# Feed-forward: late w_out tiles split one at a time, the first late piece a unit earlier, and the order of the slots' last copies

## The chip, the cores and the metric

One core of one Trainium2 chip runs the whole program; the other cores are idle. The metric is the device time of one execution in microseconds (us). The kernel before was timed three times: 435.57, 437.71 and 440.0 us, median 437.71 us.

## The reference, cut to what matters

Three layers follow one another. Sizes: batch 4, 8 heads, 768 steps, head width 48, so 3072 tokens of width 384; 32 slots (8 experts of 4), expert width 1024; network width 2048. All data are float32, and `w_in`, `w_out` of the last layer arrive as 64-bit floats.

```python
# 1 linear attention with decay, per batch and head
y[t] = r[t] @ (state + (u*k[t]) v[t]^T);  state = w * state + k[t] v[t]^T
# 2 soft mixture of experts on the tokens x (3072 x 384)
logits = x @ phi
d = softmax of logits over tokens (with + 1e-09 in the sum);  slot_input = d.T @ x
slot_out = relu(slot_input[e] @ w1[e]) @ w2[e]               # 4 slots per expert
x = (softmax of logits over slots) @ slot_out
# 3 feed-forward network with ELU
h = x @ w_in                                                 # 3072 x 2048
g = where(h > 0, h, exp(min(h, 0)) - 1)
out = g @ w_out                                              # 3072 x 384
```

## The kernel before, in words

Each engine has a queue of instructions that it works off in order. The kernel sets that order itself: the program text is the order, and semaphores are put in wherever one engine needs another's result. TensorE (PE) multiplies, VectorE (DVE) and ScalarE (ACT) do the elementwise work, GpSimd (POOL) a part of it, SyncE (SP) issues nearly all transfers.

**Attention and slots.** Tokens go by in 24 chunks of 128. Four chunks make a group, and for each of six groups `slots_a` to `slots_f` work up the logits `lg` (32 slots by 4 chunks, as 128 partitions by 128 columns): a running maximum `nmx`, the exponential `el`, its transposition back to tokens (`slots_c`, `slots_d`, giving `et`), the product with the tokens (`slots_e`, `ps_s`), and the rescaled sum `pall` (`slots_f`). The last group has its own order, `last_part` (L773). After its exponentials, `combine_a` (L792) copies the four chunk rows' running minima of `nmx` side by side (`m3`), reduces them (`mm`), copies the result back to four groups of partitions (`nm`, four copies) and lets ScalarE take `sc = exp(-nmx + nm)`. Then come the transposition `slots_c`, VectorE's copy `et`, ScalarE's copy `el` of the logits (`slots_g`), VectorE's `rb = sc * i3` (`combine_c`), the product `ps_s`, the sums `pl`, the second transposition and the combination `pi` (`combine_b`). A few filler products (`warm`) stand between them on TensorE. The experts' two products and the split of the first 10 of 16 row tiles of w_out follow.

**The network.** The slot outputs are first multiplied by w_in, so that a hidden tile is one product of the transposed slot weights `cT` with `mst` (`hid`, L1261). Work goes in 48 units. A unit is one block of 512 tokens (6 blocks) and two hidden tiles of 128: first, for all blocks, the tiles 0 to 9 (units 0 to 29), then, for all blocks, 10 to 15 (units 30 to 47). In the loop's pass n the engines get work of neighbouring units:

- TensorE: two hidden products of unit n (`hid`), the second half of the output products of unit n - 3, the first half of those of unit n - 2 (`outp`).
- ScalarE: `tanh` and `expo` of unit n, `upper` of unit n - 1, which rounds the ELU's result to `gh`.
- VectorE: `neg` of unit n, `lower` of unit n - 1 (`gl` = result less `gh`), `elu` of unit n.

The output product has three terms, `gh` by `wh`, `gh` by `wl` and `gl` by `wh` (L1306, L1307, L1309), where `wh` is a rounded tile of w_out and `wl` what rounding took away. A unit has 24 such products of 384 columns. Four PSUM tiles `fo` collect a block's rows; `leave` (L1237) takes them away when a block's last unit is done: ScalarE copies the first pass to `acc`, and in the second pass ScalarE copies to `os` and GpSimd adds, or, for the last four row tiles, VectorE adds and SP stores.

**Late pieces.** The rest of w_in and w_out is loaded and narrowed from 64 to 32 bits during the network, in 12 pieces of 384 columns, the first six of w_in, the last six w_out's tiles 10 to 15 (into `wo2`). A piece takes two units, listed in `steps` (L1359): in its first, two copies on ScalarE (`wide_a`, L314, L315) and two steps on VectorE (`wide_b1`, `wide_b2`, L318, L323); in its second, two steps on VectorE (`wide_b3`, `wide_c`, L329, L334) and two on GpSimd (`wide_d`, L337, L338), and then the load of the piece after the next. `steps` runs from unit 6, without the units in `PAUSE` (12 and 22). In unit 22 the late columns of w_in are multiplied by the slot outputs (`columns`). `SPLIT` (26, 30, 33) names the units in which two late w_out tiles are split at once (`late_split`, L1328): ScalarE's rounding `wh` (L1331) behind `upper` and the piece's copies, VectorE's subtraction `wl` (L1332) ahead of `neg`.

Of the kernel before, what the change touches and what calls it, by code (L numbers as in the profile page):

```python
# [8 lines left out]
F32 = mybir.dt.float32  # L9
# [4 lines left out]
ALU = mybir.AluOpType  # L14
# [222 lines left out]
def kernel(  # L237
# [14 lines left out]
    nc = tc.nc  # L252
    B, H, S, D = r.shape
    E, DM, FE = w1.shape
    NT = B * S
# [12 lines left out]
    FA = 10  # L268
# [28 lines left out]
    for a in range(2):  # L297
# [5 lines left out]
        out=mask, in_=mask, compare_op=ALU.is_gt, fill=0.0, base=0, pattern=[[1, 128]], channel_multiplier=-1  # L303
# [78 lines left out]
    GS = NCH // G  # L382
    nmx = const.tile([GP, GS], F32, name="nmx")
# [14 lines left out]
    with ExitStack() as actx:  # L398
# [22 lines left out]
        def warm(n):  # L421
            ps = pt_p.tile([128, 4, 128], F32, tag="pt", name="warm")
            for i in range(n):
                nc.tensor.matmul(out=ps[:, i % 4, :], lhsT=ident, rhs=ident, start=True, stop=True)
# [269 lines left out]
        def slots_a(j, copy=True):  # L694
            ps = lg[j]
            el = at3.tile([GP, 2, 128], F32, tag="el", name="el", bufs=1)
            al = at3.tile([GP, 1], F32, tag="al", name="al", bufs=2)
            lg[j], wt[j], wt[j, 1] = el, al, el[:, 1, :]
            nj = nmx[:, j:j + 1]
            if j:  # L700
                nc.vector.tensor_reduce(out=al, in_=ps[:GP], axis=AX.X, op=ALU.max)
                nc.vector.tensor_scalar(
                    out=nj, in0=al, scalar1=-1.0, scalar2=nmx[:, j - 1:j], op0=ALU.mult, op1=ALU.min
                )
            else:
                nc.vector.tensor_reduce(out=nj, in_=ps[:GP], axis=AX.X, op=ALU.max, negate=True)
            lg[j, 0] = ps
            if copy:
                slots_g(j)

        def slots_g(j):
            nc.scalar.copy(out=wt[j, 1], in_=lg[j, 0][:GP])

        def slots_b(j):
            el, ps, nj = lg[j], lg[j, 0], nmx[:, j:j + 1]
            nc.scalar.activation(out=el[:, 0, :], in_=ps[:GP], func=ACTF.Exp, bias=nj, accum_out=zz[:, j:j + 1])
            if j:
                nc.scalar.activation(out=wt[j], in_=nmx[:, j - 1:j], func=ACTF.Exp, scale=-1.0, bias=nj)

        def slots_c(j, parts=(0, 1)):  # L720
            ps = pm_p.tile([128, 2, G, NS], F32, tag="pm", name="ps_e")
            for s in parts:
                nc.tensor.transpose(
                    out=ps[:, s].rearrange("p g c -> p (g c)"), in_=lg[j][:, s, :], identity=ident[:GP, :GP]
                )
            lg[j, 2] = ps

        def slots_d(j, parts=(0, 1)):
            ps = lg.pop((j, 2))
            if 0 in parts:  # L730
                wt[j, 0] = at3.tile([128, G, NS], F32, tag="et", name="et", bufs=1)
                nc.vector.tensor_copy(out=wt[j, 0], in_=ps[:, 0])
            if 1 in parts:
                nc.scalar.copy(out=c_sb[:, G * j:G * j + G, :], in_=ps[:, 1])

        def slots_e(j):
            sp = pm_p.tile([128, DM], F32, tag="pm", name="ps_s")
            for g in range(G):
                nc.tensor.matmul(
                    out=sp[32 * g:32 * g + 32, :], lhsT=wt[j, 0][:, g, :], rhs=xs.pop(G * j + g), start=True, stop=True  # L740
                )
            lg[j, 1] = sp
# [30 lines left out]
        def last_part(j):  # L773
            slots_a(j, False)
            slots_b(j)
            combine_a()
            warm(4)
            extra()
            slots_c(j, (0,))
            warm(2)  # L780
            slots_d(j, (0,))
            slots_g(j)
            combine_c()
            slots_e(j)
            slots_f(j)
            slots_c(j, (1,))
            warm(2)
            combine_b()
            slots_d(j, (1,))


        def combine_a():  # L792
            nl = nmx[:, GS - 1:GS]
            for g in range(G):
                nc.vector.tensor_copy(out=m3[:, g:g + 1], in_=nl[32 * g:32 * g + 32, :])
            nc.vector.tensor_reduce(out=mm, in_=m3, axis=AX.X, op=ALU.min)
            for g in range(G):
                nc.vector.tensor_copy(out=nm[32 * g:32 * g + 32, :], in_=mm)
            nc.scalar.activation(out=sc, in_=nl, func=ACTF.Exp, scale=-1.0, bias=nm)

        def combine_c():
            nc.vector.tensor_scalar(out=rb, in0=i3[:GP], scalar1=sc, scalar2=None, op0=ALU.mult)

        def combine_b():
            pi = pt_p.tile([128, KD, 32], F32, tag="pt", name="pi")
            for kk in range(KD):
                nc.tensor.matmul(out=pi[:, kk, :], lhsT=pl[kk], rhs=rb, start=True, stop=True)
            nc.vector.tensor_copy(out=si, in_=pi)
            nc.vector.tensor_tensor(out=zt, in0=sc, in1=zr, op=ALU.mult)
# [74 lines left out]
        def extra():  # L884
            if extras:
                extras.pop(0)()
# [92 lines left out]
    whl = {}  # L979
# [47 lines left out]
    for a in range(2):  # L1027
        for q in range(4):
# [3 lines left out]
                out=s3, in_=s3, compare_op=ALU.is_ge, fill=0.0, base=-spe * e, pattern=[[1, NS]],  # L1032
# [3 lines left out]
                out=s3, in_=s3, compare_op=ALU.is_ge, fill=0.0, base=spe * e + spe - 1, pattern=[[-1, NS]],  # L1036
# [91 lines left out]
    whl = [[we_p.tile([128, 8, DM], F32R, tag="we", name=f"w{x}{g}") for x in "hl"] for g in range(2)]  # L1128
# [32 lines left out]
    wo2 = we_p.tile([128, FB, DM], F32, tag="we", name="wo2")  # L1161
# [28 lines left out]
    def columns(c, n):  # L1190
        return through(c, n, fo_p.tile([128, 512], F32, tag="fo", name="phm"))
# [11 lines left out]
    NPB = NPI + FB  # L1203
# [30 lines left out]
    N, NA = len(units), NB * FA // 2  # L1234
    gh, gl, po, done = {}, {}, {}, []

    def leave(n=1):  # L1237
        for _ in range(n):
            if done:
                o, r, second = done.pop(0)  # L1240
                a = acc[r // 8][:, r % 8, :]
                if not second:
                    nc.scalar.copy(out=a, in_=o)  # L1243
                    continue
                if r < NT // 128 - 4:
                    os_ = f2.tile([128, DM], F32, tag="os", name="os", bufs=4)
                    nc.scalar.copy(out=os_, in_=o)  # L1247
                    nc.gpsimd.tensor_tensor(out=a, in0=os_, in1=a, op=ALU.add)  # L1248
                else:
                    nc.vector.tensor_tensor(out=a, in0=o, in1=a, op=ALU.add)  # L1250
                nc.sync.dma_start(out=out[128 * r:128 * r + 128, :], in_=a)


# [71 lines left out]
                        term(n, i, t, (x,))  # L1325
        gh.pop(n), gl.pop(n)

    def late_split(f):  # L1328
        a, b = (t[:, f % 8:f % 8 + 2, :] for t in whl[f // 8])
        w = wo2[:, f - FA:f - FA + 2, :]  # L1330
        nc.scalar.copy(out=a, in_=w)  # L1331
        nc.vector.tensor_tensor(out=b, in0=w, in1=a.bitcast(F32), op=ALU.subtract)  # L1332

    def both(f, n, s=slice(0, 2)):
        if 0 <= n < N:
            f(n, s)
# [17 lines left out]
        upper(u, tb)  # L1354
        expo(n, tb)

    PAUSE = (12, 22)
    SPLIT = (26, 30, 33)
    steps = [n for n in range(6, N) if n not in PAUSE][:2 * NPB]  # L1359

    hid(0)
    m3, m2 = columns(1024, 128), columns(512, 256)
# [30 lines left out]
    for n in range(2, N + 3):  # L1393
        if n < N:
            hid(n)
        if n <= NARROW:
            narrow(n)
        else:
            if n == NARROW + 1:
                neg(n - 1, slice(0, 2))  # L1400
                lower(n - 2, tb)
                elu(n - 1, slice(0, 2))
            leave(1 if done and done[0][1] % 4 == 0 else 2)
            both(tanh, n)
            leave()
            both(expo, n)
            both(upper, n - 1)
            j, h = divmod(steps.index(n), 2) if n in steps else (-1, 0)
            if h == 0:
                late_wide(j, wide_a)  # L1410
            if n in SPLIT:
                late_split(FA + 2 * SPLIT.index(n))
            both(neg, n)
            both(lower, n - 1)
            both(elu, n)
            for f in (wide_b3, wide_c, wide_d) if h else (wide_b1, wide_b2):
                late_wide(j, f)
        if n < HALF:
            outp_first(n - 2, early if n == 2 else ())
        else:  # L1420
            if n > HALF:
                outp(n - 3, (2, 3))
            if n == PAUSE[1]:
                leave(2)
                m = columns(CA, CB // 2)
                for f in (high, low):
                    for i in range(2):
                        f(*m, i)
            if n - 2 < N:
                outp(n - 2, (0, 1))  # L1430
# [37 lines left out]
```

## Time and profile before

| What | Value |
|---|---|
| median of three runs | 437.71 us |
| the profiled execution's own time | 437.46 us |
| its span, first to last instruction | 435.3 us |
| mean granted clock of TensorE, share of full speed | 0.992 |
| busy TensorE, products / weight loads | 405.7 / 355.9 us |
| busy VectorE / ScalarE / GpSimd | 357.8 / 269.7 / 159.9 us |

All rows below are of this one execution, and times in them are microseconds from the start of the span. Busy time is the sum over an engine's instructions; an instruction's duration can overlap the next one's on the same engine by a little. A wait in brackets is idle time of the engine just before the row's first instruction, with the engine, tile and line that ended it.

### The profile page before, as it was taken

To read this page: it belongs to the slowest core of one execution; us is meant where nothing else is said; L and a number is where in the kernel's file an instruction comes from. 1 tells how busy PE (TensorE), PEld (TensorE's weight loads), DVE (VectorE), ACT (ScalarE), POOL (GpSimd) and SP (SyncE) were. 2 spreads that over 40 slices of the span, in tenths; PEclk is the share of its full clock that TensorE was granted. 3 is DMA by queue.
4 is the path that set the end of the run, shared out by engine and by line. 5 is a ranking of instruction groups with operands and counts; after the bars stand their busy time and mean duration, and the time that the engine had idled before them with its cause. 6 is when DMAs were issued, how large, how long until landed. Compare 5 with 4: busy or idle time off the path is not lost.

```text
span 435.3 us, 10332 instructions
## 1 busy us (share of the span) xinstructions
PE 405.7 (93%) x4177; PEld 355.9 (82%) x4177; DVE 357.8 (82%) x573; ACT 269.7 (62%) x496; POOL 159.9 (37%) x170
## 2 busy tenths in 40 slices
PE   6998989999999979988999999999999899999994
PEld 5777777787777853457989999998989889999994
DVE  5998987999899645669889999997988988777762
ACT  3654654566464411657696878776778767767750
POOL 2365655565656207200004513530314124433340
PEclk9999989999999999999999999999999999999998
DMA  8989999999998886900001111110111002111122
GB/s 155 232 267 274 250 264 259 253 285 270 289 283 252 268 273 220 356 5 0 2 0 38 36 38 36 38 44 30 38 36 38 0 2 72 56 55 48 63 75 80
DMA packets 85097, 57.44 MB, mean 132 GB/s; under 512 B 65328, under 2 KB 76848, under 8 KB 85040
## 3 DMA queue, kind: packets, MB, share of 16 engines
q1 hardware_dynamic: 84224, 56.64, 45.2%
q8 instruction: 35, 0.57, 0.6%
q14 instruction: 22, 0.18, 0.1%
q10 hardware_dynamic: 816, 0.05, 0.1%
HBM read 51.96 MB, written 4.72 MB: 130 GB/s over the span
## 4 chain that ended last, share of the span: by engine, by line
PE 65%; DVE 17%; DMA 6%; ACT 5%; issue 5%; SPq 1%; POOL 1%; DVEq 0%; ACTq 0%; POOLq 0%
PE fo L1306 12%; PE fo L1309 12%; PE fo L1307 12%; PE fh L1261 4%; PE ps_a L582 4%; DMA vd<-in_v_dram 4%; PE py L657 3%; DVE ex L1275 3%; DVE ex L1280 2%; PE pd L1070 2%; PE ph L1048 2%; DVE rT L547 2%; PE py L643 2%; PE ps_k L533 2%; PE ps_r L533 2%
## 5 line engine op out<-in xcount | busy, mean ns | idle before, releaser
L1306 PE MATMUL fo<-wh,gh 128*128 128x384 f32 x384 | 130.3, 339 | 1.5 <-ACT gh L1288 1.0
L1307 PE MATMUL fo<-wl,gh 128*128 128x384 f32 x384 | 129.8, 338 | 0.0
L1309 PE MATMUL fo<-wh,gl 128*128 128x384 f32 x384 | 125.5, 339 | 3.3 <-DVE gl L1291 3.3
L1275 DVE SCALAR_TENSOR_TENSOR ex<-ex,th 128x1024 f32<-128x1024 f32 (+1 forms) x52 | 61.1, 1174 | 20.5 <-ACT ex L1272 20.3
L1306 PEld LDWEIGHTS fo<-wh,gh 128*128 128x128 f32 x384 | 72.2, 188 | 6.0 <-ACT acc L1243 2.4
L1309 PEld LDWEIGHTS fo<-wh,gl 128*128 128x128 f32 x384 | 71.8, 188 | 4.2 <-DVE gl L1291 4.2
L1269 ACT ACTIVATE th<-fh 128x1024 f32<-128x1024 f32 (+1 forms) x53 | 50.3, 950 | 38.3 <-PE fh L1261 38.3
L1307 PEld LDWEIGHTS fo<-wl,gh 128*128 128x128 f32 x384 | 72.2, 188 | 1.8
L1291 DVE TENSOR_TENSOR gl<-ex,gh 128x1024 fp32r<-128x1024 f32 (+1 forms) x52 | 68.4, 1315 | 1.7 <-ACT gh L1288 1.3
L337 POOL TENSOR_TENSOR cv<-raw,cv 128x384 f32<-128x384 f32 x12 | 19.4, 1617 | 132.3 <-ACT gh L1288 51.2
L1280 DVE SCALAR_TENSOR_TENSOR ex<-ex,fh 128x1024 f32<-128x1024 f32 (+1 forms) x52 | 58.8, 1132 | 0.5 <-ACT ex L1272 0.4
L1272 ACT ACTIVATE ex<-fh 128x1024 f32<-128x1024 f32 (+1 forms) x53 | 50.3, 949 | 9.6 <-DVE gl L1291 9.2
L1288 ACT CAST gh<-ex 128x1024 fp32r<-128x1024 f32 (+1 forms) x52 | 51.4, 988 | 6.3 <-DVE ex L1280 4.9
L1248 POOL TENSOR_TENSOR acc<-os,acc 128x384 f32<-128x384 f32 x20 | 26.9, 1359 | 43.8 <-ACT os L1247 43.8
L631 POOL TENSOR_TENSOR bv<-vd,bs 128x384 f32<-128x384 f32 x24 | 24.3, 1011 | 39.9 <-ACT bs L626 39.9
L586 DVE TENSOR_TENSOR am<-ps_a,mask 128x512 f32<-128x512 f32 x48 | 32.5, 681 | 2.4 <-PE ps_a L582 2.1
L1261 PE MATMUL fh<-cT,mst 128*128 128x512 f32 x96 | 30.6, 400 | 1.8 <-DVE mst L1188 1.1
L582 PE MATMUL ps_a<-rT,kT 64*128 64x128 f32 x384 | 28.3, 288 | 0.3 <-ACT kT L556 0.3
L657 PE MATMUL py<-vd,am 128*64 128x48 f32 x768 | 27.8, 226 | 0.4 <-DVE am L586 0.4
L657 PEld LDWEIGHTS py<-vd,am 128*64 128x64 f32 x768 | 25.4, 142 | 0.9 <-DVE am L586 0.7
L556 ACT COPY kT<-ps_k 128x512 f32<-128x512 f32 x24 | 14.1, 586 | 18.1 <-PE ps_k L533 18.1
L582 PEld LDWEIGHTS ps_a<-rT,kT 64*128 64x128 f32 x384 | 23.7, 191 | 1.7 <-ACT kT L556 0.4
(172 smaller groups left out, 650.2 us busy)
## 6 DMA issues: line engine op xcount, KB each, us to landing
we<-in_moe_w_dram SPq DMA_DIRECT2D x14, 768.0 KB, 7.7
we<-in_moe_w_dram SPq DMA_DIRECT2D x16, 512.0 KB, 6.5
rw<-in_r_dram SPq DMA_DIRECT2D x12, 384.0 KB, 5.0
rk<-in_k_dram SPq DMA_DIRECT2D x24, 192.0 KB, 4.7
vd<-in_v_dram SPq DMA_DIRECT2D x24, 192.0 KB, 5.3
out_dram<-acc SPq DMA_DIRECT2D x24, 192.0 KB, 1.9
we<-in_moe_w_dram SPq DMA_DIRECT2D x16, 256.0 KB, 6.0
scr<-in_moe_w_out_dram SPq DMA_DIRECT2D x10, 384.0 KB, 6.1
```

What stands on the lines that cost most here:

```text
L582: nc.tensor.matmul(out=aps[a][:, p, :], lhsT=kT[q, p, :], rhs=rT[n][q, p, :], start=True, stop=True)
L657: nc.tensor.matmul(out=py[q:q + 64, h, :], lhsT=am[n, a][:, p, q:q + 64], rhs=vd[n][:, h, :], start=(c == 0), stop=(c == 0 or h == H - 1),)
L1261: nc.tensor.matmul(out=ph[n][:, i, :], lhsT=mst[(f + i) // 8][:, 128 * ((f + i) % 8):128 * ((f + i) % 8) + 128], rhs=cT[:, TB * blk:TB * b ...
L1269: nc.scalar.activation(out=th[n][:, s], in_=ph[n][:, s], func=ACTF.Tanh, scale=0.5)
L1272: nc.scalar.activation(out=ex[n][:, s], in_=ph[n][:, s], func=ACTF.Exp)
L1275: nc.vector.scalar_tensor_tensor(out=ex[n][:, s], in0=ex[n][:, s], scalar=1.0, in1=th[n][:, s], op0=ALU.add, op1=ALU.mult)
L1280: nc.vector.scalar_tensor_tensor(out=ex[n][:, s], in0=ex[n][:, s], scalar=0.0, in1=ph[n][:, s], op0=ALU.min, op1=ALU.max)
L1288: nc.scalar.copy(out=gh[n][:, s], in_=ex[n][:, s])
L1291: nc.vector.tensor_tensor(out=gl[n][:, s], in0=ex[n][:, s], in1=gh[n][:, s].bitcast(F32), op=ALU.subtract)
L1306: nc.tensor.matmul(out=o, lhsT=gh[n][:, i, s], rhs=wh, start=(f == first), stop=False)
L1307: nc.tensor.matmul(out=o, lhsT=gh[n][:, i, s], rhs=wl, start=False, stop=False)
L1309: nc.tensor.matmul(out=o, lhsT=gl[n][:, i, s], rhs=wh, start=False, stop=(f == final))
```

## The change

It has four parts. `late_split` becomes `late_high` and `late_low`, one tile each: the rounding of tiles 10 to 15 on ScalarE in units 23, 25, 27, 29, 31 and 33, the subtraction on VectorE in units 24, 26, 28, 30, 32 and 33, now behind `elu` instead of ahead of `neg`. `steps` begins at unit 5, and 7 joins the pauses, so that the first piece is worked on in units 5 and 6 instead of 6 and 7; all others stay. In `last_part` the four copies `nm` and the exponential `sc` become `combine_d`, behind the copy `et`; `slots_e` is written ahead of `combine_c`, which are on different engines. The last row tile of the output is added and stored in two halves of 192 columns, the first on SP's queue, the second on ScalarE's.

```diff
--- before.py
+++ after.py
@@ -779,9 +779,10 @@
             slots_c(j, (0,))
             warm(2)
             slots_d(j, (0,))
+            combine_d()
             slots_g(j)
+            slots_e(j)
             combine_c()
-            slots_e(j)
             slots_f(j)
             slots_c(j, (1,))
             warm(2)
@@ -794,6 +795,9 @@
             for g in range(G):
                 nc.vector.tensor_copy(out=m3[:, g:g + 1], in_=nl[32 * g:32 * g + 32, :])
             nc.vector.tensor_reduce(out=mm, in_=m3, axis=AX.X, op=ALU.min)
+
+        def combine_d():
+            nl = nmx[:, GS - 1:GS]
             for g in range(G):
                 nc.vector.tensor_copy(out=nm[32 * g:32 * g + 32, :], in_=mm)
             nc.scalar.activation(out=sc, in_=nl, func=ACTF.Exp, scale=-1.0, bias=nm)
@@ -1246,8 +1250,14 @@
                     os_ = f2.tile([128, DM], F32, tag="os", name="os", bufs=4)
                     nc.scalar.copy(out=os_, in_=o)
                     nc.gpsimd.tensor_tensor(out=a, in0=os_, in1=a, op=ALU.add)
+                elif r < NT // 128 - 1:
+                    nc.vector.tensor_tensor(out=a, in0=o, in1=a, op=ALU.add)
                 else:
-                    nc.vector.tensor_tensor(out=a, in0=o, in1=a, op=ALU.add)
+                    for i, q in enumerate((nc.sync, nc.scalar)):
+                        c = slice(DM // 2 * i, DM // 2 * i + DM // 2)
+                        nc.vector.tensor_tensor(out=a[:, c], in0=o[:, c], in1=a[:, c], op=ALU.add)
+                        q.dma_start(out=out[128 * r:128 * r + 128, c], in_=a[:, c])
+                    continue
                 nc.sync.dma_start(out=out[128 * r:128 * r + 128, :], in_=a)
 
 
@@ -1325,11 +1335,12 @@
                         term(n, i, t, (x,))
         gh.pop(n), gl.pop(n)
 
-    def late_split(f):
-        a, b = (t[:, f % 8:f % 8 + 2, :] for t in whl[f // 8])
-        w = wo2[:, f - FA:f - FA + 2, :]
-        nc.scalar.copy(out=a, in_=w)
-        nc.vector.tensor_tensor(out=b, in0=w, in1=a.bitcast(F32), op=ALU.subtract)
+    def late_high(f):
+        nc.scalar.copy(out=whl[f // 8][0][:, f % 8, :], in_=wo2[:, f - FA, :])
+
+    def late_low(f):
+        a, b = (t[:, f % 8, :] for t in whl[f // 8])
+        nc.vector.tensor_tensor(out=b, in0=wo2[:, f - FA, :], in1=a.bitcast(F32), op=ALU.subtract)
 
     def both(f, n, s=slice(0, 2)):
         if 0 <= n < N:
@@ -1354,9 +1365,10 @@
         upper(u, tb)
         expo(n, tb)
 
-    PAUSE = (12, 22)
-    SPLIT = (26, 30, 33)
-    steps = [n for n in range(6, N) if n not in PAUSE][:2 * NPB]
+    PAUSE = (7, 12, 22)
+    HIGH = (23, 25, 27, 29, 31, 33)
+    LOW = (24, 26, 28, 30, 32, 33)
+    steps = [n for n in range(5, N) if n not in PAUSE][:2 * NPB]
 
     hid(0)
     m3, m2 = columns(1024, 128), columns(512, 256)
@@ -1408,11 +1420,13 @@
             j, h = divmod(steps.index(n), 2) if n in steps else (-1, 0)
             if h == 0:
                 late_wide(j, wide_a)
-            if n in SPLIT:
-                late_split(FA + 2 * SPLIT.index(n))
+            if n in HIGH:
+                late_high(FA + HIGH.index(n))
             both(neg, n)
             both(lower, n - 1)
             both(elu, n)
+            if n in LOW:
+                late_low(FA + LOW.index(n))
             for f in (wide_b3, wide_c, wide_d) if h else (wide_b1, wide_b2):
                 late_wide(j, f)
         if n < HALF:
@@ -1420,7 +1434,7 @@
         else:
             if n > HALF:
                 outp(n - 3, (2, 3))
-            if n == PAUSE[1]:
+            if n == PAUSE[2]:
                 leave(2)
                 m = columns(CA, CB // 2)
                 for f in (high, low):
```

## Rows read from the trace of the kernel before

**Rows 1.** The waits of TensorE (PE) from 195 us on; total, times, longest.

```profile
PE fo L1309 <- DVE gl L1291: 3.3, 3, 1.2
...
PE fo L1306 <- ACT acc L1243: 0.4, 1, 0.4
```

**Rows 2.** The waits of VectorE (DVE) in the same stretch.

```profile
DVE wl L1332 <- ACT wh L1331: 5.7, 3, 1.9
```

**Rows 3.** The waits of ScalarE (ACT) in the same stretch.

```profile
ACT th L1269 <- PE fh L1261: 37.9, 35, 1.8
```

**Rows 4.** VectorE's timeline: start, us, line, operation, out<-in, count [idle before <-releaser].

```profile
311.56 1.22 DVE L1291 TENSOR_TENSOR gl<-ex,gh 128x1024 fp32r<-128x1024 f32 x1
...
316.70 1.16 DVE L1332 TENSOR_TENSOR wl<-wo,wh 128x768 fp32r<-128x768 f32 x1 [1.94 <-ACT wh L1331]
...
325.25 0.56 DVE L329 SCALAR_TENSOR_TENSOR raw<-raw,cv 128x384 int32<-128x384 int32 x1
...
326.11 1.22 DVE L1275 SCALAR_TENSOR_TENSOR ex<-ex,th 128x1024 f32<-128x1024 f32 x1
327.25 2.06 DVE L1291 TENSOR_TENSOR gl<-ex,gh 128x1024 fp32r<-128x1024 f32 x1
...
330.36 0.35 DVE L318 TENSOR_SCALAR cv<-cv 128x384 f32<-128x384 f32 x1
...
334.42 0.56 DVE L329 SCALAR_TENSOR_TENSOR raw<-raw,cv 128x384 int32<-128x384 int32 x1
...
352.90 0.96 DVE L1332 TENSOR_TENSOR wl<-wo,wh 128x768 fp32r<-128x768 f32 x1 [1.86 <-ACT wh L1331]
```

**Rows 5.** The chain that ended last, two hidden products: start, us, what.

```profile
306.91 0.46 PE fh L1261 x2
...
311.59 0.48 PE fh L1261 x2
```

**Rows 6.** VectorE's timeline, a product of the ELU beside GpSimd.

```profile
304.70 2.03 DVE L1275 SCALAR_TENSOR_TENSOR ex<-ex,th 128x1024 f32<-128x1024 f32 x1 [0.22 <-ACT ex L1272]
```

**Rows 7.** GpSimd's (POOL) timeline at that point.

```profile
304.62 1.03 POOL L337 TENSOR_TENSOR cv<-raw,cv 128x384 f32<-128x384 f32 x1 [12.18 <-ACT th L1269]
```

**Rows 8.** ScalarE's timeline around unit 6.

```profile
217.22 1.03 ACT L1269 ACTIVATE th<-fh 128x1024 f32<-128x1024 f32 x1 [1.66 <-PE fh L1261]
...
219.99 0.56 ACT L314 ACTIVATE cv<-raw 128x384 f32<-128x384 f32 x1
```

**Rows 9.** VectorE's timeline around unit 6.

```profile
219.20 1.23 DVE L1275 SCALAR_TENSOR_TENSOR ex<-ex,th 128x1024 f32<-128x1024 f32 x1 [1.20 <-ACT ex L1272]
```

**Rows 10.** The timeline of all engines at the slots' last part.

```profile
158.85 0.61 PE L424 MATMUL warm<-ident 128*128 128x128 f32 x4
158.94 0.62 DVE L798 COPY nm<-mm 32x1 f32<-32x1 f32 x4
159.59 0.29 DVE L732 COPY et<-ps_e 128x128 f32<-128x128 f32 x1
159.59 0.29 ACT L799 ACTIVATE sc<-nmx,nm 128x1 f32<-128x1 f32 x1 [0.78 <-DVE nm L798]
159.79 0.24 ACT L712 COPY el<-ps_l 128x128 f32<-128x128 f32 x1
...
159.93 0.85 PE L739 MATMUL ps_s<-x,et 128*32 128x384 f32 x8 [0.47 <-DVE et L732]
...
160.72 0.33 PE L723 MATMUL ps_e<-ident,el 128*128 128x128 f32 x1
...
160.85 0.86 DVE L752 SCALAR_TENSOR_TENSOR pl<-pall,al,ps_s 128x128 f32<-128x128 f32 x3 [0.69 <-PE ps_s L739]
```

**Rows 11.** The timeline of all engines at the end.

```profile
429.74 0.56 DVE L1250 TENSOR_TENSOR acc<-fo,acc 128x384 f32<-128x384 f32 x1 [0.50 <-PE fo L1309]
```

**Rows 12.** DMA issues: line, queue, operation, count, KB each, median us to landing.

```profile
out_dram<-acc SPq DMA_DIRECT2D x24, 192.0 KB, 1.9
...
phi_sb<-in_moe_phi_dram ACTq DMA_DIRECT2D x1, 48.0 KB, 4.2
```

## The prediction

> **What bounds the kernel.** Read the list of TensorE's waits first, from the start of the feed-forward network: its product stream is the clock of that stage, and only what holds it up counts. Two waits stand after the warm-up of the pipeline: three for `gl`, 3.3 us together, and one of 0.4 us for a copied-out accumulator [rows 1]. Then ask what made `gl` late. VectorE waited 5.7 us in three places for `wh`, ScalarE's rounding of two w_out tiles, issued in the same unit just ahead of VectorE's subtraction [rows 2]; one such wait, ahead of 316.70, is 1.94 us, with the subtraction of 768 columns behind it [rows 4]. ScalarE in turn waited 37.9 us in 35 places for TensorE [rows 3], so it has room, about 1.1 us in most units. VectorE has hardly any. Hidden products follow one another by 4.68 us [rows 5], so TensorE takes 9.36 us for a pair of units, while VectorE, on the same steps of two successive pieces, takes from 325.25 to 334.42, 9.17 us [rows 4]. Elsewhere (the last group of the slots) TensorE is idle for 0.47 us, on VectorE's copy `et` [rows 10].
>
> **Late w_out tiles.** Three pairs of (round, subtract) become six singles; the rounding goes into units 23 to 33 (odd), the subtraction a unit later, behind `elu`, the last two tiles' into 32 and 33. So VectorE finds `wh` done long before and the 5.7 us of waiting go. The rounding itself is ScalarE's: 0.48 us or so at half the columns, every second unit, in units without the two copies of a piece; cover is its waiting [rows 3]. If that cover were gone it would delay `ex`, which VectorE reads.
> What is late next? VectorE's own work. Instructions back to back overlap by 0.08 us (326.11 plus 1.22 against 327.25), so 768 columns undisturbed cost 0.96 less 0.08, 0.88 [rows 4]; half of the columns' part plus the fixed part I put at 0.47 us. Bounds: 0.44, half, and 0.56, the full duration of a 384-column addition out of PSUM [rows 11]. 0.47 is nearer to the same operation. A pair of units then takes VectorE 9.64 us against 9.36: a debt of 0.28 per pair, repaid from a lead.
> The lead: the subtraction `gl` of unit 24 ends at 311.56 + 1.22 = 312.78. TensorE runs, per unit, two hidden products (0.47) and 24 others, (4.68 - 0.47)/24 = 0.175 each; before it wants this `gl` it has two hidden products, the 12 of the second half of unit 23 and two with `gh` to do: 311.59 + 0.48 + 14 x 0.175 = 314.52 [rows 4, 5]. Lead 1.74, and 1.27 behind the first new single. To the next `gl` VectorE needs 1.13 (`elu`), 0.86 (piece), 1.14 and, beside GpSimd, 1.98, 5.11 in all [rows 4]: lead 0.84 in unit 25. Every pair takes 0.28, so 0.56, 0.28 and 0.00 in units 27, 29, 31: TensorE is just not held up. Unit 32 has no piece: 1.13 + 0.47 + 2 x 1.14 = 3.88, lead 0.80. The last single, f = 15, comes behind the `elu` after it, 1.60 later, while TensorE wants it 0.35 later: 0.80 + 0.35 - 1.60 = -0.45. So about 0.5 of the 3.3 us stays, as a wait for `wl` in unit 34, and **2.8 us** are gained (2.3 with singles at 0.56; 3.3 with nothing left).
> The Trainium skill (VectorE: DVE Perf Modes, "The TRN2 errata — SBUF-src ops pay a fixed extra latency per instruction") speaks against splitting: each extra instruction pays a fixed term of 58 cycles at 0.96 GHz, by another measurement there 151. As an estimate from that page the three extra subtractions would cost 0.18 to 0.47 us together, and the sum would be 0.0 to 0.3 us worse than mine. The trace's 0.06 each (twice 0.47 against 0.88) lies at the low end.
>
> **First piece in unit 5.** Its two copies (219.99, about 0.9 us) leave unit 6's queue on ScalarE, where tanh, exponential, rounding and accumulator copies run back to back until TensorE has waited 0.4 us [rows 1, 8]. In unit 5 they find the 1.66 us in which ScalarE waits ahead of 217.22 [rows 8], and the clamp and shift on VectorE, 0.7 us, the 1.20 us ahead of 219.20 [rows 9]. The other steps move from 7 to 6, GpSimd's too, and unit 7 becomes empty; the next load on SP's queue is issued a unit earlier, in front of nothing. The copy TensorE waits for comes 0.9 us earlier, so **0.4 us**. Bounds 0 (GpSimd beside `gl` now in unit 6 to 7, up to 0.84 later) and 0.45.
>
> **Slots.** The four `nm` copies (0.62 us) no longer stand ahead of `et`. The transposed block's product is over by about 159.05, so `et` runs from there to 159.35, and TensorE's filler products end at 158.85 + 0.61 = 159.46: `ps_s` starts 0.47 us earlier [rows 10]. But `nm` now ends at 159.97, so `sc` starts 0.4 us later on ScalarE, with the copy `el` queued behind it. That copy ends near 160.45 instead of 160.03, and the second transpose, which before followed at 160.72, starts at 160.49. `rb` waits for `sc` and stands ahead of `pl` on VectorE: `pl` at 160.55 instead of 160.85 [rows 10]. So 0.25 to 0.3 of 0.47 are left; I take **0.25**. Bounds: 0.47, and a loss of 0.2 if `et` can't start before 159.5. No later stage up to the network waits on a transfer, so this moves the end.
>
> **Last output.** One addition of 0.56 us [rows 11] and one store, landing in 1.9 us [rows 12], become two halves on two queues. The first store leaves some 0.2 us earlier, the second, on ScalarE's queue, up to 0.5 later with half of the bytes. The nearest row is the same store; the only row of ScalarE's queue that I keep is a load at the busy start, 4.2 us [rows 12]. I take **0**; bounds a gain of 0.3 and a loss of 2.3. By the Trainium skill (DMA: Bandwidth & Descriptors, "Issuing engines are not separate DMA queues") a second issuing engine saves the sequencer's time and no more; no run here shows it.
>
> **Sum.** 2.8 + 0.4 + 0.25 + 0 = 3.45 us. The profiled execution took 437.46, its span 435.3 and 2.16 around it; 437.46 - 3.45 = **434.0**. The median of the runs, 437.71, is 0.25 above that execution, so I leave the number.
>
> **Rivals.** (a) *The debt is larger.* VectorE's instruction `neg` took 2.03 instead of 1.22 where GpSimd's product began first, at 304.62 against 304.70 [rows 4, 6, 7]: 0.81 more. If that happens in two of the four pairs from 26 on and singles cost 0.56 (six times 0.09), the residue is 0.5 + 0.5 + 1.6 = 2.6, and 0.7 + 0.65 is gained: **436.1**. For it: VectorE's margin is 3%. Against: where VectorE is late it doesn't wait for `ex`, and `neg` gets in first, as at 326.11.
> (b) *Slower: GpSimd first in every pair.* In units 26, 28, 30 and 32, 4 x 0.81, the residue is 0.5 + 0.5 + 3.2 = 4.2, more than the 3.3 of before: 437.46 + 0.9 - 0.65 = **437.7**, and 438.4 if the two small gains fail. It decides once a pair costs 0.8 us more; it needs `ex` to come after the piece's last step in every pair. Against: `ex` can start when the `gl` two units before is done, 2.0 us before VectorE is ready, and takes 1.0. The Trainium skill (SBUF — State Buffer, "Who interferes with whom") says that the one of VectorE and GpSimd that starts first holds their shared pair of ports and the other blocks. The slowed `neg` agrees.
> (c) *Nothing left over.* No residue, 0.45, 0.47, and 0.3 at the end: 4.5 us, **432.9**.
> (d) *The rounding isn't ahead*: ScalarE's copy sits behind an exponential that waits for VectorE, and a third of the waits return. Gain 1.9 + 0.65 - 0.5, **435.4**.
>
> **Chances.** Forecast 0.55, its own range 433.2 to 435.2; (a) 0.18, (b) 0.07, (c) 0.12, (d) 0.08. A measurement of this kernel tells about 1% from no change; the three runs lie between 435.57 and 440.0. 1% under the median is 433.3: most of (c) and the lower fifth to quarter of the forecast, with scatter, give 0.27 for faster. Slower by 1% (442.1) no case reaches; a loss on ScalarE's store on top of (b), and scatter, 0.04. The range 432.3 to 437.0 leaves out (b), a part of (a) and the lower edge of (c).
>
> **What would show it.** VectorE without a wait for `wh`; six subtractions of 0.47 to 0.56 us; no wait for `gl` from unit 26 on, one of about 0.5 us for `wl` in unit 34; the 0.4 us at unit 8 gone; `ps_s` half a microsecond after `mm`, and the network's start 0.25 earlier; the end as far behind the last product as before. Wrong if `neg` after a piece takes 2 us again and again, if the waits for `gl` come back, or if the store on ScalarE's queue lands late.

## The result: 431.3 us, 1.0% less, and the profile after

Over 20 runs each the kernel before took 436.04 us (median) and the changed one 431.3; the ratio is 0.9897, 95% interval 0.9877 to 0.9918, so 4.5 us less (3.6 to 5.4; the medians alone differ by 4.7). The forecast was 3.45 us less and 434.0 us, with a range down to 432.3; the measured time lies 1.0 us below it. Two things are in that miss. The execution whose rows were read, 437.46 us, stood 1.4 us above what proved to be the median of before; and the terms of the sum were too small, by about 1 us together. The profiled execution of the changed kernel took 430.51 us, its span is 428.7.

The first lines of its page:

```profile
span 428.7 us, 10335 instructions
## 1 busy us (share of the span) xinstructions
PE 404.3 (94%) x4177; PEld 355.0 (83%) x4177; DVE 358.0 (84%) x577; ACT 270.6 (63%) x499; POOL 162.6 (38%) x170
```

VectorE's work is the same within 0.2 us, and so is TensorE's within 1.4: less waiting, not less work. TensorE's waits from 210 to 365 us, where before the list was that of [rows 1]:

```profile
PE fo L1317 <- DVE wl L1343: 0.2, 1, 0.2
```

The three waits for `gl` and the one for the accumulator copy are gone from this list; the wait for the last tile's `wl` that the prediction put into unit 34 is there. VectorE's wait for `wh` [rows 2] stands nowhere in its list. The list of the weight loads (PEld), which the prediction did not read, keeps waits for accumulator copies, here from 195 us on, before and after:

```profile
PEld fo L1306 <- ACT acc L1243: 2.4, 4, 0.9
PEld fo L1316 <- ACT acc L1247: 1.5, 4, 0.6
```

Spans of two executions shouldn't be subtracted here, since the attention stage, which the change doesn't touch, differs by more than some of the parts: its end, the reduction `al` of the last group, began at 157.54 us in the profile before and at 155.18 after, and between 154.41 and 156.23 in the eight other kernels below. TensorE's granted clock shows a dip in that stage before (0.91 from 60 to 80 us, of which it was 0.51, near the lower level of 1.2 GHz, from 62.9 to 66.4; 1.00 in the other stretches of 20 us); the other nine kernels have none there. So each stage is taken by itself, from the start of one named instruction to the start of another. In the table "slots" goes from `al` to the first expert product `ph`, the unit columns from one unit's hidden product to another's, and "end" from the last output product to the end of the span, which is known to a tenth, so that this column is good to 0.05 us.

| Kernel | slots | `ph` to unit 8 | 8 to 24 | 24 to 35 | 35 to 47 | end |
|---|---|---|---|---|---|---|
| before | 4.99 | 61.33 | 78.20 | 55.99 | 56.25 | 5.93 |
| changed | 4.58 | 61.28 | 77.52 | 52.21 | 56.23 | 6.64 |
| e1_only_late | 4.99 | 61.33 | 78.22 | 52.26 | 56.25 | 5.92 |
| e2_no_late | 4.57 | 61.27 | 77.55 | 56.02 | 56.23 | 6.03 |
| e3_one_store | 4.57 | 61.28 | 77.56 | 52.24 | 56.24 | 6.01 |
| e4_pairs_ahead | 4.99 | 61.33 | 78.20 | 52.64 | 56.24 | 5.98 |
| e5_f15_first | 4.58 | 61.27 | 77.56 | 51.81 | 56.24 | 5.96 |
| e6_best | 4.57 | 61.92 | 77.54 | 51.78 | 56.24 | 6.02 |
| e7_same_unit | 4.58 | 61.90 | 77.57 | 59.01 | 56.23 | 6.17 |
| e8_low_after_piece | 4.57 | 61.28 | 77.56 | 55.63 | 56.25 | 6.44 |

The columns repeat to 0.05 us wherever the code of the stage is the same, except the end, and 0.6 us in e6 and e7 ahead of unit 8. Those are the clock: from 195 to 200 us it was granted at 0.66 in both, at 1.00 in the changed kernel with one store and tile 15 first (e5), which loses nothing there; output products are recorded for 0.52 us instead of 0.34 while it is at its lower level. TensorE had just idled 1.08 us for `mst`, but so it had in e5, so why it fell stays open. From e6, the busy times of a window with the granted clock third from the end, and a product of TensorE's timeline:

```profile
195.00:200.00 5.00, 4.36 (x15) 4.16 (x16) 4.79 (x10) 3.71 (x8) 0.00 (x0) 0.66 0.00 0
...
196.53 0.52 PE L1310 MATMUL fo<-wh,gh 128*128 128x384 f32 x1
```

From the table the change gains 0.41 in the slots, 0.68 with the first piece, 3.78 with the late tiles, 4.9 us in all, and loses some at the end. That agrees with the measured 4.5 as far as its interval can tell, and the close agreement is in part luck: the device time also holds about 2.1 us outside the span in the kernel before and 1.9 in the changed one (medians of 41 and 20 executions), a difference of 0.25 us that stands in no stage.

**Why the waits understated the stalls.** TensorE's timeline of the kernel before at the first wait for `gl`:

```profile
318.87 0.34 PE L1307 MATMUL fo<-wl,gh 128*128 128x384 f32 x1
320.19 0.45 PE L1309 MATMUL fo<-wh,gl 128*128 128x384 f32 x1 [0.99 <-DVE gl L1291]
320.47 0.34 PE L1306 MATMUL fo<-wh,gh 128*128 128x384 f32 x1
```

A product is recorded for 0.34 us, but in an unbroken stream the next starts 0.175 later. From 318.87 to 320.19 are 1.32 us, 1.14 too much, and to the next 0.28, 0.10 too much: 1.25 us lost, 0.99 recorded. So it is at the accumulator copy:

```profile
223.86 0.63 PE L1261 MATMUL fh<-cT,mst 128*128 128x512 f32 x2
224.94 0.45 PE L1306 MATMUL fo<-wh,gh 128*128 128x384 f32 x1 [0.45 <-ACT acc L1243]
225.23 0.34 PE L1307 MATMUL fo<-wl,gh 128*128 128x384 f32 x1
```

Two hidden products take 0.47, here 1.08, and 0.29 follow instead of 0.175: 0.72 us lost, 0.45 recorded. Over units 24 to 35 the loss before is 55.99 less 11 x 4.687 (the spacing of an unbroken unit, 56.24/12), 51.56: 4.43 us, not 3.3. The three stalls for `gl` are 4.1 of it (1.25, 1.50 and 1.34 by the starts of the products). The rest, 0.36 us from unit 28 to 29, is a fourth stall, for an accumulator copy, that TensorE's own list does not have; it shows on a weight load:

```profile
322.78 0.19 PEld L1306 LDWEIGHTS fo<-wh,gh 128*128 128x128 f32 x1 [0.53 <-ACT acc L1243]
```

**VectorE in units 24 to 34, after the change** (start, us, line, operation):

```profile
301.20 2.03 DVE L1285 SCALAR_TENSOR_TENSOR ex<-ex,th 128x1024 f32<-128x1024 f32 x1 [0.21 <-ACT ex L1282]
...
306.26 0.54 DVE L1343 TENSOR_TENSOR wl<-wo,wh 128x384 fp32r<-128x384 f32 x1
306.73 0.34 DVE L318 TENSOR_SCALAR cv<-cv 128x384 f32<-128x384 f32 x1
...
315.89 0.54 DVE L1343 TENSOR_TENSOR wl<-wo,wh 128x384 fp32r<-128x384 f32 x1
...
321.28 1.22 DVE L1285 SCALAR_TENSOR_TENSOR ex<-ex,th 128x1024 f32<-128x1024 f32 x1
322.41 2.05 DVE L1301 TENSOR_TENSOR gl<-ex,gh 128x1024 fp32r<-128x1024 f32 x1
...
348.65 0.55 DVE L1343 TENSOR_TENSOR wl<-wo,wh 128x384 fp32r<-128x384 f32 x1
```

Each single takes 0.47 us from start to start, as costed (by full duration 0.54). From single to single, 306.26 to 315.89, a pair of units takes 9.63 us against the 9.64 worked out. Only the first `neg` met GpSimd's product first (2.03, as in [rows 6]); from then on, in the units with GpSimd's products, `neg` starts ahead of them and takes 1.22, and `gl` behind it 2.05, the order of [rows 4]. GpSimd's product beside the `neg` at 321.28:

```profile
321.49 1.89 POOL L337 TENSOR_TENSOR cv<-raw,cv 128x384 f32<-128x384 f32 x1 [5.76 <-issue]
```

VectorE runs into its debt as forecast, and the last single is what TensorE meets:

```profile
348.76 0.34 PE L1316 MATMUL fo<-wh,gh 128*128 128x384 f32 x1
349.26 0.44 PE L1317 MATMUL fo<-wl,gh 128*128 128x384 f32 x1 [0.16 <-DVE wl L1343]
349.54 0.34 PE L1319 MATMUL fo<-wh,gl 128*128 128x384 f32 x1
```

0.50 and 0.28 instead of 0.175 each are 0.43 us lost; 0.45 was the forecast's. A second loss, in no step of the prediction, is 0.22 us from unit 28 to 29, where the kernel before lost 0.36. It shows only in the weight loads and on ScalarE:

```profile
317.89 0.19 PEld L1316 LDWEIGHTS fo<-wh,gh 128*128 128x128 f32 x1 [0.39 <-ACT acc L1247]
```

```profile
316.95 0.51 ACT L1339 CAST wh<-wo 128x384 fp32r<-128x384 f32 x1
317.36 0.85 ACT L1247 COPY acc<-fo 128x384 f32<-128x384 f32 x2
```

The rounding of tile 12 stands ahead of the two accumulator copies at a block's end, and the output product that needs their PSUM tiles waits. The two runs without a rounding in unit 27 (e4 and e6 below) lose nothing from 28 to 29: 4.69 and 4.68 us.

**The slots after** (all engines):

```profile
156.70 0.29 DVE L732 COPY et<-ps_e 128x128 f32<-128x128 f32 x1 [0.15 <-PE ps_e L723]
156.90 0.61 DVE L802 COPY nm<-mm 32x1 f32<-32x1 f32 x4
157.04 0.16 PEld L739 LDWEIGHTS ps_s<-x,et 128*32 128x32 f32 x8
157.04 0.85 PE L739 MATMUL ps_s<-x,et 128*32 128x384 f32 x8
157.54 0.29 ACT L803 ACTIVATE sc<-nmx,nm 128x1 f32<-128x1 f32 x1 [1.08 <-DVE nm L802]
157.74 0.25 ACT L712 COPY el<-ps_l 128x128 f32<-128x128 f32 x1
157.87 0.24 DVE L806 TENSOR_SCALAR rb<-i,sc 128x32 f32<-128x32 f32 x1 [0.36 <-ACT sc L803]
158.02 0.86 DVE L752 SCALAR_TENSOR_TENSOR pl<-pall,al,ps_s 128x128 f32<-128x128 f32 x3
158.04 0.14 PEld L723 LDWEIGHTS ps_e<-ident,el 128*128 128x128 f32 x1 [0.84 <-ACT el L712]
```

Add 2.36 (157.54 less 155.18) to compare with [rows 10]: `et` at 159.06, forecast 159.05; `ps_s` at 159.40, forecast 159.46; `sc` at 159.90, later by 0.31 and not 0.4; `pl` at 160.38, forecast 160.55, before 160.85.

**The end.** Additions and stores of the last row tile:

```profile
422.44 0.62 DVE L1258 TENSOR_TENSOR acc<-fo,acc 128x192 f32<-128x192 f32 x2 [0.50 <-PE fo L1319]
422.86 0.33 SPq L1259 DMA_DIRECT2D out_dram<-acc  x1
423.09 0.38 ACTq L1259 DMA_DIRECT2D out_dram<-acc  x1
```

### The profile page after: what moved, and what is told of

It reads as the page before. It is cut to its first block, busy times and chain, and to the rows that moved or that the text cites. A ratio compares the mean times of both kernels' runs of the same rounds, so it can differ in the third digit from the quotient of the medians.

```text
span 428.7 us, 10335 instructions
## 1 busy us (share of the span) xinstructions
PE 404.3 (94%) x4177; PEld 355.0 (83%) x4177; DVE 358.0 (84%) x577; ACT 270.6 (63%) x499; POOL 162.6 (38%) x170
## 4 chain that ended last, share of the span: by engine, by line
PE 64%; DVE 19%; DMA 7%; issue 6%; ACT 2%; POOL 1%; SPq 0%; ACTq 0%; DVEq 0%; POOLq 0%
PE fo L1317 12%; PE fo L1316 12%; PE fo L1319 12%; PE fh L1271 4%; PE ps_a L582 4%; DVE ex L1290 3%; DMA vd<-in_v_dram 3%; PE py L657 3%; DMA scr<-in_moe_w_out_dram 3%; DVE ex L1285 3%; DVE rT L547 3%; PE pd L1074 2%; PE ph L1052 2%; DVE am L586 2%; PE py L643 2%
## 5 line engine op out<-in xcount | busy, mean ns | idle before, releaser
L657 PE MATMUL py<-vd,am 128*64 128x48 f32 x768 | 26.9, 222 | 0.4 <-DVE am L586 0.4
L678 ACT COPY xT<-ps_x 128x384 f32<-128x384 f32 x24 | 11.5, 478 | 22.0 <-PE ps_x L676 22.0
```

The costliest lines, as they stand in the source:

```text
L657: nc.tensor.matmul(out=py[q:q + 64, h, :], lhsT=am[n, a][:, p, q:q + 64], rhs=vd[n][:, h, :], start=(c == 0), stop=(c == 0 or h == H - 1),)
```

## The experiments

Each ratio is to the kernel before, timed beside the run: median 435.01 us for e1 to e4, 435.75 us for e5 to e8. Code cuts show the lines that matter; ` ...` marks a gap.

**The late tiles alone.** (e1_only_late) The kernel before with the first part of the change.

```diff
-            if n in SPLIT:
-                late_split(FA + 2 * SPLIT.index(n))
+            if n in HIGH:
+                late_high(FA + HIGH.index(n))
 ...
             both(elu, n)
+            if n in LOW:
+                late_low(FA + LOW.index(n))
```

> The kernel before with the singles of the late w_out tiles alone (round a unit ahead, subtract behind elu). Theory: a recorded wait understates what a stall costs TensorE, since a product is recorded for 0.34 us but the next follows after 0.175; the cost is the spacing of products, 4.4 us for the three stalls of before, and some 0.6 stays. From the hidden product of unit 24 to that of unit 35 it should take 52.2 us instead of 56.0, and the time should fall by 3.8 us, ratio 0.991. Rival: the recorded 3.3 us are the whole cost and the rest of the gain came from other stages: 53.0 us for that stretch, time lower by 2.8 to 3.0 us, ratio 0.993 to 0.994.

Ratio 0.9927 (0.9901 to 0.9952), 3.2 us less (2.1 to 4.3). Units 24 to 35 take 52.26 us, 3.73 less than before: the theory's number. The interval of the time holds both; the stretch decides it, and the recorded waits are not the whole cost. One part of the theory is off: the three stalls are 4.1 of its 4.4 us, and the rest is the accumulator copy from unit 28 to 29.

**All but the late tiles.** (e2_no_late) The changed kernel with `late_split` in units 26, 30 and 33 again.

```diff
-    HIGH = (23, 25, 27, 29, 31, 33)
-    LOW = (24, 26, 28, 30, 32, 33)
+    SPLIT = (26, 30, 33)
```

> The changed kernel with the late tiles split in pairs in units 26, 30 and 33 as before; first piece in unit 5, the slots' order and the two half stores stay. Theory: slots give 0.4 us, the piece 0.7 (the gap of unit 8 to 9 falls from 5.4 to 4.7 us between hidden products, though only 0.45 was recorded as a wait), the stores take 0.7 back: time lower by 0.4 us, ratio 0.999; the three waits for gl are back at about 1.0 to 1.2 us each. Rival (recorded waits are the cost, stores cost nothing): 0.25 + 0.45, lower by 0.7 us, ratio 0.998.

Ratio 0.998 (0.9961 to 1.0), 0.9 us less (0 to 1.7): the rival's number, in an interval that holds the theory's too, so the stages decide. The recorded waits are the old ones:

```profile
PE fo L1319 <- DVE gl L1301: 3.3, 3, 1.2
```

Units 24 to 35 take 56.02. The slots give 0.42, units 8 to 24 0.65, of which only 0.45 was recorded. On the stores this profile goes against the theory: end 6.03 with the halves, 0.1 more than before, not 0.7.

**One last store.** (e3_one_store) The changed kernel without the halves.

```diff
-                elif r < NT // 128 - 1:
-                    nc.vector.tensor_tensor(out=a, in0=o, in1=a, op=ALU.add)
                 else:
-                    for i, q in enumerate((nc.sync, nc.scalar)):
-                        ...
+                    nc.vector.tensor_tensor(out=a, in0=o, in1=a, op=ALU.add)
                 nc.sync.dma_start(out=out[128 * r:128 * r + 128, :], in_=a)
```

> The changed kernel with the last row tile added and stored in one piece on SP's queue, as before. Theory: the half stores landed after 3.3 us each and the second left later, so one store ends 0.7 us sooner: last product to end of span 5.9 us instead of 6.6, ratio to the kernel before 0.988. Rival: the last store of any form lands in about 3 us, and the 0.7 us are scatter of one execution: 6.4 to 6.8 us.

Ratio 0.9899 (0.9874 to 0.9925), as the changed kernel's 0.9897: no difference seen in the time. The end is 6.01 us, near the theory's 5.9, but half of its reason is gone: a store in one piece can land as late, this kernel's last after 3.3 us. Over the profiles the end is 5.92 to 6.02 with one store (six) and 6.03, 6.17, 6.44, 6.64 with halves (four): some 0.35 us for the halves on average, less than the theory's 0.7. To 0.05 us the lowest of the four is not told apart from the highest of the six, and no time shows the loss; what makes it stays open.

**Pairs, but ahead.** (e4_pairs_ahead) The kernel before, with tiles rounded and subtracted two at a time, ahead.

```diff
-    SPLIT = (26, 30, 33)
+    HIGH = (25, 29, 33)
+    LOW = (26, 30, 33)
 ...
-                late_split(FA + 2 * SPLIT.index(n))
+                late_high(FA + 2 * HIGH.index(n))
 ...
+                late_low(FA + 2 * LOW.index(n))
```

> The kernel before with the tiles still rounded and subtracted in pairs of 768 columns, but rounded in units 25, 29 and 33 and subtracted behind elu in units 26, 30 and 33. Theory: what cost time was VectorE's waiting for ScalarE in front of neg, not the size of the instruction, so pairs ahead gain nearly as much: no wait for gl, one of 0.3 to 0.9 us for the last wl, time lower by 3.3 to 3.8 us, ratio 0.991 to 0.9925. Rival: splitting into singles is what keeps gl on time; with 0.88 us in one unit gl comes late in units 26 and 30 again, 0.3 to 0.6 us each, and half of the gain is lost, ratio 0.995.

Ratio 0.9919 (0.9903 to 0.9936), 3.5 us less. Units 24 to 35 in 52.64, 3.35 of the 3.78 us, with one wait left, for the last `wl`:

```profile
PE fo L1307 <- DVE wl L1333: 0.7, 1, 0.7
```

So the theory: the gain comes without smaller instructions. Singles gain 0.65 us more at the last tiles and lose the 0.22 from unit 28 to 29, 0.4 in all. But two things were changed at once, the rounding's unit and the subtraction's place behind `elu`, and no run has one without the other for all tiles. The last pair has its rounding and its subtraction in the same unit 33, and there the place alone was enough: `wh` is done 1.56 us before `wl` begins, which does not wait (ScalarE, then VectorE).

```profile
346.16 0.84 ACT L1329 CAST wh<-wo 128x768 fp32r<-128x768 f32 x1
...
348.56 0.95 DVE L1333 TENSOR_TENSOR wl<-wo,wh 128x768 fp32r<-128x768 f32 x1
```

As an estimate from [rows 4], `neg`, `lower` and `elu` ahead of the subtraction are 3 x 1.14, 3.4 us, more than the 1.9 that VectorE waited. So which of the two the other tiles need is not shown.

**Singles, but not ahead.** (e7_same_unit) The changed kernel, with each tile rounded and subtracted in one unit, ahead of `neg`.

```diff
-            if n in HIGH:
-                late_high(FA + HIGH.index(n))
+            if n in LOW:
+                late_high(FA + LOW.index(n))
+                late_low(FA + LOW.index(n))
             both(neg, n)
 ...
-            if n in LOW:
-                late_low(FA + LOW.index(n))
```

> The changed kernel with singles that are not ahead: rounding and subtraction of one tile both in units 24, 26, 28, 30, 32 and 33, the subtraction in front of neg as in the kernel before. Theory: VectorE's waiting for ScalarE in the same unit is the cost, so six waits of 1.4 to 1.6 us in place of three of 1.9 make it worse than before: units 24 to 35 in 57.6 us (56.0 before, 52.2 changed), slower than the changed kernel by about 5 us, ratio to before 1.002. Rival: smaller instructions are what helps: 53 to 54 us.

Ratio 1.0047 (1.0023 to 1.007), 2.0 us slower than before. Units 24 to 35 take 59.01 us, 1.4 more than the theory had. VectorE's wait, from 285 to 365 us:

```profile
DVE wl L1343 <- ACT wh L1339: 9.6, 6, 2.5
```

Six waits of 1.6 us on average in place of three of 1.9; three of the six subtractions, beside GpSimd, also took 1.07 to 1.08 us instead of 0.55. Singles by themselves are worse than pairs.

**GpSimd first.** (e8_low_after_piece) The changed kernel with the subtractions behind the piece's last step, so that GpSimd's product is under way when `neg` comes.

```diff
-    LOW = (24, 26, 28, 30, 32, 33)
+    LOW = (25, 27, 29, 31, 32, 33)
 ...
+            for f in (wide_b3, wide_c, wide_d) if h else (wide_b1, wide_b2):
+                late_wide(j, f)
             if n in LOW:
                 late_low(FA + LOW.index(n))
-            for f in (wide_b3, wide_c, wide_d) if h else (wide_b1, wide_b2):
-                late_wide(j, f)
```

> The changed kernel with the subtractions of tiles 10 to 13 behind the piece's last step in units 25, 27, 29 and 31, so that GpSimd's first product starts ahead of the neg that follows. It tests the price of the rivals (a) and (b) of the prediction. Theory (whichever starts first keeps the shared port): GpSimd is first in every pair, neg takes 2.0 us instead of 1.2 there, gl still 2.05, 0.8 us more a pair, so that units 24 to 35 take 52.2 + 4 x 0.8 - 1.1 to 52.2 + 4 x 0.8, 54.3 to 55.4 us. Rival: the order of the start doesn't matter to the sum of the two: 52.2 us as in the changed kernel.

Ratio 0.995 (0.9928 to 0.9971). Units 24 to 35 take 55.63, 3.4 more than in the changed kernel and just above the expected upper end. VectorE and GpSimd in one of the pairs:

```profile
322.74 0.55 DVE L1343 TENSOR_TENSOR wl<-wo,wh 128x384 fp32r<-128x384 f32 x1
323.21 2.07 DVE L1285 SCALAR_TENSOR_TENSOR ex<-ex,th 128x1024 f32<-128x1024 f32 x1
325.20 2.06 DVE L1301 TENSOR_TENSOR gl<-ex,gh 128x1024 fp32r<-128x1024 f32 x1
```

```profile
322.96 1.24 POOL L337 TENSOR_TENSOR cv<-raw,cv 128x384 f32<-128x384 f32 x1 [7.28 <-ACT ex L1282]
324.28 1.90 POOL L338 TENSOR_TENSOR wo<-raw,cv 128x384 f32<-128x384 f32 x1
```

`neg` takes 2.05 to 2.07 instead of 1.22 in all four pairs, and the stretch grows by 3.4 us, 0.85 a pair. That is the price of rivals (a) and (b), 0.81 a pair in the prediction. (By the ratios the kernel is 2.3 us slower than the changed one; their intervals leave room for 3.4.) It wasn't paid in the changed kernel because VectorE, the late engine there, starts `neg` directly behind the piece, 0.21 us ahead of GpSimd's product. The trace agrees with the Trainium skill (SBUF — State Buffer, "Who interferes with whom"): who starts first keeps the shared ports, and the other waits.

**The two losses that were left.** (e5_f15_first, e6_best) First, in the kernel with one store, tile 15's subtraction ahead of `elu`; then also tile 12's rounding a unit later.

```diff
+            if n == LOW[-1]:
+                late_low(FT - 1)
             both(elu, n)
-            if n in LOW:
+            if n in LOW[:-1]:
                 late_low(FA + LOW.index(n))
```

> The changed kernel with one last store and the subtraction of tile 15 ahead of elu in unit 33 instead of behind it. Theory: the 0.43 us by which units 34 to 35 are apart too long (5.11 against 4.68) come from that subtraction being 1.13 us too late, so they go: units 24 to 35 in 51.8 us instead of 52.2. Rival: the tile's rounding on ScalarE, issued in the same unit, is what is late, and VectorE now waits for it ahead of elu: 52.2 us or more.

Ratio 0.9876 (0.9841 to 0.991), 429.32 us, the fastest median of the study. The stretch takes 51.81, as expected; no product's wait is left in its list there, and the 0.25 us over 51.56 are those of units 28 to 29, where this run lost 0.24. It is 0.40 us better than the changed kernel there and by 0.35 or so at the end; the intervals of the two ratios overlap, so the times alone don't show it.

```diff
-    HIGH = (23, 25, 27, 29, 31, 33)
+    HIGH = (23, 25, 28, 29, 31, 33)
```

> As the run with tile 15 first, and the rounding of tile 12 put into unit 28 behind the piece's copies instead of unit 27. Theory: the 0.22 us too much of units 28 to 29 (4.91 against 4.69) come from that rounding standing ahead of the two accumulator copies on ScalarE, so they go too: units 24 to 35 in 51.6 us, which is eleven times 4.69, and the time is 0.6 us under the changed kernel's, ratio to the kernel before 0.988. Rival: with the rounding in unit 28 the exponential of unit 29 comes late and VectorE waits: 52 us or more.

Neither came true. Ratio 0.9892 (0.9854 to 0.9931), and the stretch takes 51.78. Units 28 to 29 are 4.68 us apart now, but 33 to 34 4.92, with the same form of wait at the next block's end:

```profile
342.50 0.19 PEld L1310 LDWEIGHTS fo<-wh,gh 128*128 128x128 f32 x1 [0.35 <-ACT acc L1247]
```

The theory was right on the place and wrong on the gain. In ScalarE's order the next block's two copies stand behind an exponential and a rounding to `gh`, and that exponential waited for VectorE (0.27 us); it seems that TensorE, no longer held up in one block, meets the copies in the next, which no further run tests:

```profile
339.89 1.03 ACT L1276 ACTIVATE ex<-fh 128x1024 f32<-128x1024 f32 x1 [0.27 <-DVE gl L1295]
341.02 1.05 ACT L1292 CAST gh<-ex 128x1024 fp32r<-128x1024 f32 x1
341.98 0.86 ACT L1247 COPY acc<-fo 128x384 f32<-128x384 f32 x2
```

## Why the prediction was right and wrong

- **What bounds the kernel:** right in kind. VectorE's waiting for the rounding made `gl` late; e4 and e7 separate that from the size of the instruction. The step that failed stands here: it took TensorE's recorded waits, 3.3 and 0.4 us, as what the stalls cost. By the spacing of products these stalls cost 4.1 and 0.7 us, and a fourth, 0.36 us for an accumulator copy in the same stretch, is not in that list at all.
- **Late w_out tiles:** the mechanism was right to the instruction, the size too small: 3.78 us instead of 2.8, and above the upper bound of 3.3, which was the recorded wait. VectorE's debt (9.63 against 9.64 a pair), the price of a single (0.47), the wait for `gl` that just doesn't come and the wait for `wl` in unit 34 (0.43 against 0.45) are as worked out. By spacing, the same working would have given 4.1 - 0.5 = 3.6; the rest is that the fourth stall fell from 0.36 to 0.22 us. Wrong was that the rounding costs nothing: it costs these 0.22 us, where accumulator copies follow it.
- **The Trainium skill's fixed cost of an instruction** (VectorE: DVE Perf Modes, "The TRN2 errata — SBUF-src ops pay a fixed extra latency per instruction"): twice 0.47 against 0.87 (start to start of a pair's subtraction in e4) is 0.07 us more per split pair. The measurement, near the low end of that page's terms, decides.
- **First piece in unit 5:** 0.68 instead of 0.4, above its bound of 0.45, by the same error; e1 and e2 hold the part apart.
- **Slots:** 0.41 instead of 0.25, within its bounds. Mis-sized was the delay of `sc` (0.31, not 0.4), because `nm` starts 0.20 behind `et`, not 0.3, and so of `pl`.
- **Last output:** taken as 0, between bounds; about -0.35, with losses of 0.1 to 0.7 in single executions. That the halves would land no sooner was not foreseen: the 1.9 us of [rows 12] are the median of 24 stores, and the last one of the kernel before landed after 3.0, the two halves in the profile after 3.3. The prediction's own sign of being wrong, a late store on ScalarE's queue, came.
- **The sum:** 3.45 forecast; 0.41 + 0.68 + 3.78 - 0.35 = 4.5 by stages, and 4.5 measured (3.6 to 5.4). The late tiles' term is 1.0 too small, the two others 0.4 together, and the stores take 0.35 back.
- **The base:** the range started from one execution and a median of three, 437.71. Seventeen more runs put the median at 436.04. Scatter was used for the chances, but its effect on the base itself was left out of the lower end: 436.04 - 3.45 would have been 432.6. Either error alone would have left the time inside the range (437.46 - 4.5 is 433.0); it took both. The execution that was read has the longest attention stage of the ten profiles, by 1.3 us; that this makes up most of its 1.4 above the median is likely, and not shown.
- **Rivals:** (a) and (b) had the right price (e8: 0.85 a pair) and, as argued against them, the wrong order. (c), nothing left over, is nearest in the time, 432.9, and its gain of 4.5 us is the measured one, but by luck: 0.65 us was left over in the stretch and 0.35 lost at the end, where it had a gain, and the stalls cost more than its 3.3. (d) did not occur.

## What to carry to other kernels

Price a stall of TensorE by the starts of its products against the spacing of an unbroken stream; here the recorded wait and the lost time differ by 0.26 to 0.27 us each time, a fifth to two thirds of the stall, and stalls of 0.36 and 0.22 us have no recorded wait on the products at all: read the weight loads' waits too. When one engine waits for another inside a step, first put distance between the two (the producer a step ahead, the consumer later in its step) before making the pieces smaller: pairs with distance gained 3.35 of 3.78 us, singles without it cost 3.0. Sum an engine's work per pair of steps and its lead; in a saturated engine that arithmetic held to 0.01 us per pair.

## What the runs showed of the hardware that was not expected

A product that follows a stall is itself recorded longer (0.44 or 0.45 instead of 0.34 us) and the next starts 0.28 instead of 0.175 behind it, so that a stall of TensorE costs about 0.10 us after its end. And the last store lands later than its like: most of the 192 KB stores land after 1.9 us, the last one, in the six kernels that store it whole, after 2.7 to 3.3, and the two halves of 96 KB, on either queue, after 2.8 to 3.3 us. A few earlier ones, most of them from 370 to 380 us, take 2.4 to 3.4 as well. What delays the last one stays open.
